# Attention and a gated MLP on one core: the weight guard on DVE, small work between DVE and GpSimd, and a new written-out order

## The chip, the cores and the metric

One Trainium2 chip, one of its cores. The metric is the device time of one execution in microseconds (us), the median of several runs. Engines are named as in the profile: PE (TensorE, matmuls; PEld its weight loads), DVE (VectorE), ACT (ScalarE), POOL (GpSimd), SP (SyncE, which issues nearly all DMAs).

## The reference

Inputs are q, k, v of shape (8, 12, 448, 64) and the weights of a gated MLP. Per batch and head:

```
q_n = q / sqrt(mean(q*q) + 1e-6) * g_q         (k likewise)
s = q_n @ k_n.T / 8;  p = exp(s - max(s));  p = p / (sum(p) + 1e-9);  a = p @ v
```

The 12 heads of a batch are laid side by side as x (448, 768). Then, per batch:

```
h = gelu_tanh(x @ w_in)                        w_in (768, 1024);  u, v = halves of h
v_n = (v - mean) / sqrt(var + 1e-6) * g_ln
out = x + (u * (w_sg @ v_n + b_sg)) @ w_out    w_sg (448, 448), w_out (512, 768)
```

The weights `w_in` and `w_out` arrive as pairs of 32-bit words, the two halves of a 64-bit float, and are decoded to fp32 on the chip.

## The kernel before

**Stages.** The kernel walks over 48 pairs of heads (`pv`, index `i`) in 24 units of four heads (index `u`). For a unit, `norms` squares q and k on ScalarE and sums them on DVE; `split` scales them on GpSimd (for unit 0 on DVE) and splits each into a high and a low fp16 half (`hl`), and two DMA transposes write them as `qt`. `scores` then makes seven score tiles for the unit, 168 in all: matmuls into a PSUM tile `s` (two buffers), the negative maximum `nm` on DVE, two exponentials on ScalarE with their sums, a fp16 high half on ScalarE (`ahl`), the low half on DVE (`ahl`, which frees the PSUM tile), and a DMA transpose into `at`. `recips` (L446) turns the sums of a pair into reciprocals: an addition of 1e-9 on DVE (`rx`, L453), the reciprocal on DVE (`ry`), and two fp16 halves on GpSimd (`rh`, `rl`). `pv` lets PE spread these over a row (`row`), multiplies attention and values, scales by the row and splits the result into fp16 halves `x`.

**Weights.** `weights` (L281) loads `w_in` in 12 pieces of 128x512 and `w_out` in 8 of 128x384. Each goes through `decode` (L259): on DVE a shift of the high word (L263) and two instructions that bring in sign and low word; on ScalarE the square of the high word read as fp32; on GpSimd a comparison of this square with a least value and a multiplication of the decoded value by the result, the guard (L267, L268). Then `w_in` is squared on ScalarE for a common scale, scaled, copied to fp16 on GpSimd, and the fp16 low part is taken on DVE (L297).

**MLP.** After each sixth pair, `moe` (for the last batch `tail`) runs the two products with `w_in`, the two gelu clusters, `layernorm` (L543), the product with `w_sg`, the gating and the product with `w_out`. `layernorm` takes the statistics on DVE and finds 1/sqrt(var + 1e-6) on DVE with a guess by integer arithmetic (2 instructions) and `newton` (7), for four columns at once.

**The order.** No engine chooses its order while running. Every operation is recorded as one entry of a plan (matmuls that belong together as one), and `Plan.emit` issues the entries in the sequence that the packed string `ORDER` gives; it was searched beforehand. Each engine, and SP's DMA queue, then works through its own instructions strictly in that order.

Of the kernel before, what the change touches and what calls it, by code (L numbers as in the profile page):

```python
# [22 lines left out]
LEAST_SQ = (1.125 * 2.0 ** -15) ** 2  # L23
# [18 lines left out]
    "44sv#i{-cJqB(la0x2|cUgl6Kp!{Ntf5o|nd(OvXHbk@MwZk^-0$+rgq~cJgI{Ey1d;QntUzWsXq|R-%d+O(ZHDK!(rKW-4RG3kfwWQ(tyCYLiZQ"
    "-gq!ubzZ^wNF2JSdZ&aoaQ@)haN@QtFs`SM}Xr^vxE=s?%Pu)!U}?wl6KM!qP1w!n4HTTcvR+7UOOKZXJ{2*i^FVW?n$4?n%1^D~^82jZK}hn*xy"
    "``@Y!GJu;NduP$A`djQW)G`!*_>>BmYld%m2BU&|qC&u2^=Z0{GC1><`VHz>)?_WMQ=Iia7hbIgi&HkMin(aR_QxyUX;aQZboe4KE&ae5<N5gVLV"
    "&i{Uw=<sKxvAHt&CK9TmbPn`q#g14xcKicJr=+J7U;6nv|*$%Kg8$s$S=0uQAK_qIj_*k<7IO69|9LsBs~*@c!%cVq4|TquHRoByx`+2J2L{d@67"
    "bAikS8B=~Jdz2TLoj9rXE=-+#Dlk8`MA-0i#&ocy5UO5?ios<|G?sq0F|t5$DRIs7L$#1xqkIsM<e&fhCobqIiujtnZ$Z+A{OI`E~PCWl_}=;+eI"
    "fe}mB1;wd8_47R&CemdA3r}U*>m%<zirwoJqRy+HoVO|cxNn4ZU*f9mzZ-^+ylv75V{B4JUbpJk|5nD=W&Wv_{Sv=VnpBeb%~j!#4ONM;qsq%w^!"
    "V*VW%ugb4QpbuLN3l3`!6Y$x-fr0b&IQGMZ2Ya(wKxfF70WrqB~g&s?(*t<3T8}i7c#Biy}+&@Lw&{-Ilg3$KJOP6XHZx1xzQwQgCe9G4Sb+OQaL"
    "4G_PpOE(@c5cY80P9niKy7qAr=rbVN2Zfdg%Gz@KeqkCwz<6|jIDAQ$25rz7!b{pI8HwP8z*n&ZVra%A#*&H^IEueL5%oXrRQ|ZAEyBeR+7@sh-V"
    "9?bdd4RFZw;+7{j~zppD>2#O#_4H~#K9J(%W+aBEk<_P86Q@>Z{Nv3_`IOSzC+-G3q%%x>;Suc%m1FbWTnAheAn_J%l|aTNjMVg(9{pqPfu~JyLc"  # L50
    "j{w?&;ZU<ZA$q4we&w>khEUjf?b#n}xnT>f)B*>ZHrj^jm9X`V|zll6=`%d#u<q6f$LF;8@hKNo_YJbACoxgzDO0_%oI<|!YT<@wt0!hivW@X{8`"
# [835 lines left out]
```

## Time and profile before

| | us |
|---|---|
| median of 3 runs (lowest to highest) | 948.27 (947.92 to 949.22) |
| the profiled execution | 948.41 |
| its span, first to last instruction | 946.6 |
| outside the span | 1.81 |

The mean granted TensorE clock was 0.949 of full speed over the span. "Busy" counts an engine's instructions alone, not its waits; an idle time is put down to the releaser that came last. The helper that records the operations stands at one line, L122, which is why nearly every row has that line: instructions are told apart by their tiles.

### The profile page before, as it was taken

The page shows a single profiled execution, that of the slowest core. Times are in us where ns is not written, and L with a number is a line of the kernel's source. Part 1 is how long each engine was busy: PE and PEld are TensorE (multiplying, and loading weights), DVE is VectorE, ACT ScalarE, POOL GpSimd, SP SyncE. Part 2 cuts the span into 40 slices and gives each one's busy share as a digit, 9 for nine tenths or more (in the row PEclk, how much of TensorE's full clock was granted, in tenths as well). Part 3 has the DMA queues.
Part 4 walks back from the last instruction along what each step waited for, and adds up shares of the span by engine and source line. Part 5 has one row for each costly group of instructions (what it writes and reads, how often), then busy time and mean ns, then how long its engine had stood idle before and what let it go on. Part 6 is the DMA issues. An engine that isn't in the chain of part 4 may idle for free.

```text
span 946.6 us, 16618 instructions
## 1 busy us (share of the span) xinstructions
PE 771.6 (82%) x5908; PEld 422.9 (45%) x5908; DVE 677.1 (72%) x1046; ACT 664.4 (70%) x1374; POOL 566.8 (60%) x669
## 2 busy tenths in 40 slices
PE   0124565797998888999898889989897999999997
PEld 0002231343454335644473347534563466444757
DVE  4988988868777786748967768559867776765052
ACT  3468866877778779767887589667877787884231
POOL 5997989885946587453865576714955762104100
PEclk9999777897899998999999899989999999999999
DMA  8966799986899889987889479959897698752102
GB/s 219 243 153 137 161 229 216 197 171 131 167 207 221 165 168 189 194 192 147 192 174 211 108 164 216 219 97 196 179 208 166 119 202 185 158 114 44 50 1 68
DMA packets 448003, 155.69 MB, mean 164 GB/s; under 512 B 404336, under 2 KB 441776, under 8 KB 447920
## 3 DMA queue, kind: packets, MB, share of 16 engines
q1 hardware_dynamic: 447344, 154.18, 76.8%
q8 instruction: 46, 0.75, 0.3%
q10 hardware_dynamic: 576, 0.46, 0.2%
q14 instruction: 37, 0.30, 0.1%
HBM read 43.57 MB, written 11.01 MB: 58 GB/s over the span
## 4 chain that ended last, share of the span: by engine, by line
PE 31%; DVE 20%; ACT 16%; POOL 12%; DMA 9%; issue 8%; SPq 4%; POOLq 0%; ACTq 0%; DVEq 0%
PE pv L122 6%; ACT s L122 5%; DVE ahl L122 4%; DVE nm L122 4%; PE s L122 4%; SPq L122 4%; DMA qt<-hl 3%; ACT ahl L122 3%; POOL qk L122 2%; POOL hl L122 2%; PE acc L122 2%; DVE vl L122 2%; ACT sqk L122 2%; DMA at<-ahl 2%; DMA qk<-in_q_dram 2%
## 5 line engine op out<-in xcount | busy, mean ns | idle before, releaser
L122 ACT ACTIVATE s<-s,nm 128x448 f32<-128x448 f32 x336 | 203.8, 607 | 73.2 <-DVE nm L122 68.5
L122 DVE TENSOR_TENSOR ahl<-s,ahl 128x896 f16<-128x896 f32 x168 | 181.9, 1085 | 69.3 <-ACT ahl L122 68.3
L122 DVE TENSOR_REDUCE nm<-s 128x2 f32<-128x896 f32 x168 | 180.9, 1085 | 41.2 <-PE s L122 40.1
L122 PE MATMUL s<-qt 64*128 64x448 f16 (+1 forms) x1152 | 134.7, 378 | 69.4 <-DVE ahl L122 58.2
L122 ACT ACTIVATE ahl<-s 128x896 f16<-128x896 f32 x168 | 153.4, 917 | 2.4
L122 PE MATMUL pv<-at,vh 128*64 128x448 f16 (+1 forms) x672 | 128.9, 382 | 18.3 <-DMA at<-ahl 7.2
L122 PEld LDWEIGHTS <-vh 128*64 128x64 f16 (+2 forms) x928 | 67.1, 110 | 113.1 <-issue 66.7
L122 PEld LDWEIGHTS <-x 128*128 128x128 f16 (+1 forms) x1056 | 74.6, 103 | 78.8 <-issue 28.8
L122 PEld LDWEIGHTS <-qt 64*128 64x128 f16 (+1 forms) x1152 | 43.1, 100 | 139.2 <-issue 95.3
L122 POOL CAST vh<-vr 128x512 f16<-128x512 f32 x48 | 30.6, 640 | 96.9 <-PE pv L122 88.6
L122 POOL TENSOR_TENSOR hl<-qk,hl 128x896 f16<-128x896 f32 x46 | 87.2, 1900 | 1.1
L122 PEld LDWEIGHTS <-wi 128*128 128x128 f16 x576 | 54.8, 99 | 61.4 <-issue 15.8
L122 POOL TENSOR_TENSOR qk<-qk,ny 128x896 f32<-128x896 f32 x46 | 78.3, 1716 | 1.6
L122 PE MATMUL pv<-at,vl 128*64 128x448 f16 (+1 forms) x336 | 74.4, 380 | 0.0
L122 POOL TENSOR_TENSOR qk<-qk,gg 128x896 f32<-128x896 f32 x23 | 49.2, 2139 | 33.3 <-ACT sqk L122 33.1
L122 DVE TENSOR_REDUCE ss<-sqk 128x14 f32<-128x896 f32 x48 | 51.8, 1079 | 21.4 <-ACT sqk L122 21.1
L122 POOL TENSOR_TENSOR gt<-gt,u 128x448 f32<-128x448 f32 x30 | 33.9, 1147 | 54.6 <-DVE gt L122 51.0
L122 ACT ACTIVATION_READ_ACCUMULATOR s<-s,nm 128x1 f32 x336 | 66.4, 198 | 0.0
L122 ACT ACTIVATE sqk<-qk 128x896 f32<-128x896 f32 x48 | 45.5, 949 | 29.7 <-DMA qk<-in_k_dram 9.0
L122 POOL CAST rh<-ry 128x8 f16<-128x8 f32 x48 | 10.5, 220 | 82.7 <-DVE ry L122 47.3
L122 POOL CAST hl<-qk 128x896 f16<-128x896 f32 x48 | 46.3, 971 | 22.1 <-DMA qt<-hl 20.3
L122 POOL TENSOR_TENSOR vl<-vr,vh 128x512 f16<-128x512 f32 x48 | 56.9, 1185 | 2.2
(834 smaller groups left out, 1747.1 us busy)
## 6 DMA issues: line engine op xcount, KB each, us to landing
out_dram<-ot SPq DMA_DIRECT2D x56, 192.0 KB, 3.0
wo_h<-in_moe_w_in_dram SPq DMA_DIRECT2D x12, 512.0 KB, 6.5
vr<-in_v_dram SPq DMA_DIRECT2D x32, 192.0 KB, 3.4
qk<-in_q_dram SPq DMA_DIRECT2D x47, 128.0 KB, 3.0
qk<-in_k_dram SPq DMA_DIRECT2D x47, 128.0 KB, 2.9
vr<-in_v_dram SPq DMA_DIRECT2D x32, 144.0 KB, 3.4
qk<-in_q_dram SPq DMA_DIRECT2D x47, 96.0 KB, 2.8
qk<-in_k_dram SPq DMA_DIRECT2D x47, 96.0 KB, 2.7
```

Of the source, the lines that this page charges most:

```text
L122: return lambda *args, **kw: self.plan.add(lambda: f(*args, **kw))
```

## The change

- `decode`: ScalarE writes the absolute value of the high word (as fp32) to the destination; a new DVE instruction takes the maximum of it and a least value; the shift then reads this result in place. The two GpSimd instructions and the square are gone.
- `w_in`'s fp16 low parts are taken on GpSimd instead of DVE (6 instructions of 128x1024).
- The addition of 1e-9 to the sums is on GpSimd instead of DVE (48 of 128x8).
- `layernorm`, except in the last batch: ScalarE's logarithm and exponential, then one step of four DVE instructions, in place of the guess and `newton`.
- `ORDER` is another sequence, for 3977 entries where there were 4018.

```diff
-LEAST_SQ = (1.125 * 2.0 ** -15) ** 2
+LEAST = 1.125 * 2.0 ** -15
 ORDER = (
...
-    def decode(dst, raw, tmp):
+    def decode(dst, raw):
         hi, lo = raw[:, :, 1], raw[:, :, 0]
-        di = dst.bitcast(I32)
-        V.tensor_scalar(out=di, in0=hi, scalar1=3, scalar2=0x3FFFFFF8, op0=ALU.logical_shift_left, op1=ALU.bitwise_and)
+        di, x = dst.bitcast(I32), raw.bitcast(F32)[:, :, 1]
+        A.activation(out=dst, in_=x, func=AF.Abs)
+        V.tensor_scalar(out=dst, in0=dst, scalar1=LEAST, scalar2=None, op0=ALU.max)
+        V.tensor_scalar(out=di, in0=di, scalar1=3, scalar2=0x3FFFFFF8, op0=ALU.logical_shift_left, op1=ALU.bitwise_and)
         V.scalar_tensor_tensor(out=di, in0=hi, scalar=-0x40000000, in1=di, op0=ALU.bitwise_and, op1=ALU.bitwise_or)
         V.scalar_tensor_tensor(out=di, in0=lo, scalar=29, in1=di, op0=ALU.logical_shift_right, op1=ALU.bitwise_or)
-        A.activation(out=tmp, in_=raw.bitcast(F32)[:, :, 1], func=AF.Square)
-        G.tensor_scalar(out=tmp, in0=tmp, scalar1=LEAST_SQ, scalar2=None, op0=ALU.is_ge)
-        G.tensor_tensor(out=dst, in0=dst, in1=tmp, op=ALU.mult)
...
-            V.tensor_tensor(out=wi[:, t, 1], in0=tmp, in1=wi[:, t, 0], op=ALU.subtract)
+            G.tensor_tensor(out=wi[:, t, 1], in0=tmp, in1=wi[:, t, 0], op=ALU.subtract)
...
-        V.tensor_scalar(out=x, in0=sums, scalar1=1e-9, scalar2=None, op0=ALU.add)
+        G.tensor_scalar(out=x, in0=sums, scalar1=1e-9, scalar2=None, op0=ALU.add)
...
-        rsqrt_guess(y, si, x)
-        newton(y, x, tt)
+        if not last:
+            A.activation(out=tt, in_=x, func=AF.Ln)
+            A.activation(out=y, in_=tt, func=AF.Exp, scale=-0.5)
+            V.tensor_tensor(out=tt, in0=x, in1=y, op=ALU.mult)
+            V.tensor_tensor(out=tt, in0=tt, in1=y, op=ALU.mult)
+            V.tensor_scalar(out=tt, in0=tt, scalar1=-0.5, scalar2=1.5, op0=ALU.mult, op1=ALU.add)
+            V.tensor_tensor(out=y, in0=tt, in1=y, op=ALU.mult)
+        else:
+            rsqrt_guess(y, sml.tile([P, CK], I32, name="li", bufs=2), x)
+            newton(y, x, tt)
```

Unpacked, the two orders put these recorded instructions ahead of some landmarks on the engine named (in brackets: how many of them belong to the decoding of the weights or its splits):

| landmark | before | after |
|---|---|---|
| GpSimd, last low half of q and k of the second unit | 64 (29) | 19 (0) |
| GpSimd, last low half of q and k of the third unit | 88 | 52 |
| DVE, first maximum `nm` | 55 (33) | 39 (24) |
| DVE, low half of the 7th score tile | 116 (44) | 95 (52) |
| DVE, low half of the 14th score tile | 144 (52) | 151 (57) |
| DVE, low half of the 21st score tile | 179 (60) | 179 (68) |
| DVE, low half of the 28th score tile | 229 (66) | 230 (80) |
| PE, score tiles ahead of the first product of the first MLP | 10 | 12 |
| PE, score tiles ahead of the first output product of the first MLP | 38 | 39 |

The number of DMA issues on SP's queue is the same, 571 recorded.

## Rows read from the trace of the kernel before

**Rows 1.** The page's first part, of the whole span: engine, busy us (share of the span), instructions.

```profile
PE 771.6 (82%) x5908; PEld 422.9 (45%) x5908; DVE 677.1 (72%) x1046; ACT 664.4 (70%) x1374; POOL 566.8 (60%) x669
```

**Rows 2.** Busy time by stretch: from and to in us from the span's start, its length, then for PE, PE's weight loads, DVE, ACT (ScalarE) and POOL (GpSimd) the busy us (instructions), the granted TensorE clock, the share of the DMA engines, GB/s.

```profile
0.00:250.00 250.00, 129.58 (x903) 57.21 (x905) 203.42 (x288) 170.14 (x356) 205.19 (x218) 0.87 0.87 185
250.00:850.00 600.00, 553.25 (x4407) 306.21 (x4405) 438.98 (x673) 464.69 (x966) 345.48 (x432) 0.97 0.83 175
850.00:947.00 97.00, 88.81 (x604) 59.44 (x600) 34.68 (x85) 29.61 (x55) 16.13 (x20) 0.99 0.19 45
```

**Rows 3.** What PE waited for from 0 to 250 us, the two longest that are used: engine, tile, the releaser, us in total, times, the longest.

```profile
PE s L122 <- DVE ahl L122: 42.4, 18, 10.5
PE s L122 <- DMA qt<-hl: 10.8, 1, 10.8
```

**Rows 4.** The same from 250 to 850 us.

```profile
PE s L122 <- DVE ahl L122: 15.7, 17, 3.4
PE row L122 <- POOL rh L122: 6.9, 4, 3.7
PE sw__1368 L122 <- DVE mv L122: 3.4, 1, 3.4
```

**Rows 5.** What DVE waited for from 0 to 250 us, the two longest.

```profile
DVE ss L122 <- ACT sqk L122: 13.2, 6, 5.0
DVE ahl L122 <- ACT ahl L122: 8.2, 11, 1.5
```

**Rows 6.** ScalarE's squares of the decoded halves of `w_in`, from the groups of instructions by shape: line, engine, operation, out<-in, shapes, count | busy us, mean ns | idle us before them and its releasers.

```profile
L122 ACT ACTIVATE wo_l<-wi 128x512 f32<-128x512 f32 x12 | 7.6, 630 | 21.2 <-POOL wi L122 21.2
```

**Rows 7.** Three pieces of the chain that ended last, between 60 and 100 us: start us, us, what.

```profile
65.08 1.50 POOL wo_l L122
78.92 1.84 POOL hl L122
80.79 5.34 DMA qt<-hl
```

**Rows 8.** DVE's and ScalarE's work on the maxima `nm` by stretch; DVE's count in brackets is the number of score tiles: length, DVE busy (count), ACT busy (count), clock, DMA share, GB/s.

```profile
0.00:250.00 250.00, 40.62 (x38) 53.72 (x151) 0.87 0.87 185
250.00:850.00 600.00, 139.24 (x129) 184.35 (x515) 0.97 0.83 175
```

**Rows 9.** GpSimd's groups of instructions by shape, those of the guard first; columns as in the group of ScalarE's squares.

```profile
L122 POOL TENSOR_SCALAR wo_l<-wo_l 128x512 f32<-128x512 f32 x12 | 18.5, 1538 | 10.9 <-DVE wi L122 9.9 <-ACT wo_l L122 0.2
L122 POOL TENSOR_TENSOR wi<-wi,wo_l 128x512 f32<-128x512 f32 x12 | 17.8, 1483 | 1.9 <-DVE wi L122 0.8 <-DVE nt L122 0.6
L122 POOL TENSOR_SCALAR sqo<-sqo 128x384 f32<-128x384 f32 x8 | 10.2, 1275 | 5.9 <-ACT sqo L122 5.4
L122 POOL TENSOR_TENSOR wr<-wr,sqo 128x384 f32<-128x384 f32 x8 | 8.0, 1002 | 4.0 <-DVE wr L122 3.8
L122 POOL TENSOR_TENSOR vl<-vr,vh 128x512 f16<-128x512 f32 x48 | 56.9, 1185 | 2.2
L122 POOL TENSOR_SCALAR nx<-ss 128x28 f32<-128x28 f32 x23 | 5.6, 242 | 5.3 <-DVE ss L122 3.6
```

**Rows 10.** DVE's groups by shape: the decode's shift (TENSOR_SCALAR) for both weights, the low parts of `w_in`, the addition of 1e-9.

```profile
L122 DVE TENSOR_SCALAR wi<-wo_h 128x512 int32<-128x512 int32 x12 | 7.3, 612 | 5.8 <-DMA wo_h<-in_moe_w_in_dram 5.8
L122 DVE TENSOR_SCALAR wr<-rawo 128x384 int32<-128x384 int32 x8 | 8.5, 1067 | 2.5 <-POOL bb L122 2.0 <-POOL wo_l L122 0.4 <-DMA rawo<-in_moe_w_out_dram 0.2
L122 DVE TENSOR_TENSOR wi<-wo_l,wi 128x1024 f16<-128x1024 f32 x6 | 7.9, 1326 | 0.0
L122 DVE TENSOR_SCALAR rx<-sums 128x8 f32<-128x8 f32 x48 | 23.0, 480 | 12.2 <-ACT s L122 12.0
```

**Rows 11.** Two lines of the answers on the tiles `wr` and `rx`: count, then shortest/median/longest in ns, first and last start in us, forms.

```profile
L122 DVE TENSOR_SCALAR wr<-rawo x8: 356/948/2219, 48.4 to 170.9; 128x384 int32<-128x384 int32 x8
L122 DVE TENSOR_SCALAR rx<-sums x48: 158/172/2858, 75.1 to 853.5; 128x8 f32<-128x8 f32 x48
```

**Rows 12.** Small instructions of the layernorm root on DVE, and the logarithm of the norms on ScalarE, from the groups by shape.

```profile
L122 DVE TENSOR_TENSOR lt<-lt,ly 128x4 f32<-128x4 f32 x16 | 4.0, 250 | 0.3
L122 DVE SCALAR_TENSOR_TENSOR ly<-lt,ly 128x4 f32<-128x4 f32 x16 | 2.6, 160 | 0.4
L122 ACT ACTIVATE nt<-nx 128x28 f32<-128x28 f32 x24 | 5.3, 221 | 9.1 <-POOL nx L122 8.9
```

**Rows 13.** Who waited for the reciprocals' two fp16 halves, whole span: PE's weight loads and PE.

```profile
PEld L122 <- POOL rh L122: 14.4, 9, 4.1
PEld L122 <- POOL rl L122: 8.3, 20, 1.9
PE row L122 <- POOL rh L122: 9.7, 7, 3.7
```

More of the change, by code (lines that the diff above doesn't have):

```diff
@@ L42 @@
[L42 to L51, printed above, removed]
@@ L97 @@
[L97 to L100 removed]
+    "c-m!G2V7Lw(!b}HU3wMiAfN~cxF86k2(}m%5i6S5dt%gRjCpy<_nBvsm(Lh`ml#W8F9^10iw!}ME+8OXK&97ZcW-;A+$Hb*KDKc8+&Ob*{xkERxh"
@@ new lines @@
+    "Cp~*J$<av7k$37I&I4*NRI{m`o`cdiR5rgkd?1e-UHRv;3G}xfoC;K8;ChlxIC|k>@)d`TcjsbH@x1)%IDJ!NT7GIQx<9p#{RZGat_vW+W~fd;i1"
+    "KPxj5^2h^AfbCPGkSHFV^YJ+cg3z)Vj?IZw8CMANo=fUMM_GjX|(%;!FocD9ax#_8AFOR%oz93<Lx*_G#+tew~bctOLA}=m_C|}t9ELOi(IBfUF^"
+    "h;oBiY)h9O;w#(e}2-R^qA!%ovy6VrVRC}4(P2;Tcy|4r_E<8(iT^FmwVPmd#Fwh9Bz^1xAz~D?zudkR9?qAue_EkaCMiz(D+Z-x8PZg_Qj!fY!L"
+    "feyZdxzh+k#mCMF^3tH4$3fM&q!1(~M~fV5HI>mli*3jG%Sk$6!knOg08%6dxVYoCkh)`R7c0^is3q_YdkP7Tq}FF1MLX_*E-Ro)@oS-^T$Qa+VF"
+    "Lz8Ll`PS-Oso=-RZOxRd+WKqd|0P+>`Cqr%q4Sa!9B=#Em!<<&d^>=y5`X&2v&v@c*IuQADm@#4!M#OveHqx;33UD(O&3}B=uHMOg@fO@9T{QoUe"
@@ new lines @@
+    "T}G-tg5i&@@<*W`3ucamw1ZwQ7jjySfn)JMwTqW0h5-V`pUaFQ0ASyg#G>d~!H6*Uay^cI<<wyr}z5-Wi*A#5^9wNhTc=pA?4jl$KR<_hLDaHPoc"
+    "N?ERFW;%ieZ9!8palmu*>*1|_L>P%CHIot_%JCmqyv$oVWrYEwOX4`b1|IngRb8vJp=&}-7Ak07C%-JMfXsvXzu+7?@BvpjXW{#%J?zps2bupnd="
+    "&F!%Y2WGv3CT&z<2qL?KF8;lcFaA$LVdu#6<8!*p0ywrxYgSYD!FQL=v?}~tD2VTt0%9`yy6CS&35O6dR<CP<j-I6yW+Vi%Nkt4rl5P@4Xn5y`?q"
+    "&XVttdweL282ZTp`StWP{O=?c_)J(f&Qf3)@M@e{tR8}$9%ypWQ{@3)*<Fgi^;v3&J+(YMV{EFV#zJ+$eY6*9APlYNBu0as0mjg3ZPQtU^ky0x2b"
+    "{^`iZ^<TQL-@AT`)_pzr-pY4!S&EL1$P3kr=0JR|9+ErjW)LrM>by{yc9sX3+{+HTIA{EI&w+nVPO*IP^^Md?PbT;G-8J0t`V`0Pg7Bcmffco5pB"
@@ new lines @@
+    "g;gc)Yo^kUzJf-Ed}Zw;dC;a<0>!MS^6w0_HFPFnSi8PV8_v7w1;P0`m@z1%T74fK9j7^PR0p&4q<BcYL9Bk9{M@v*w)?XC>&ZnjAa4n?=E-Gd#n"
+    "-Q{AtL?Pb&kvo1qa9?+<A{mVN?@{5m`Xo`M3QR2@QJQx?umkFAD_U^_!m4A^q+z@i+&Nxw%v#jXH%_UdAP7cWfv-!e`Qok8LZPmXrMDRa;anmEzB"
+    "rD|y!;jwrA#a4kjwSX@8LtB(q~}rKN&F3YRQgETs-q~#>b7N2c-Eu1^bjCCjrA|d4z|8&)f#)quV3fnZT@odO1bmqN0vK2<4tvquEUmW*uARJyDE"
+    "8x^E;2-GwqW;J+vllX~MLn3HGgYTuww96Y$yLTL~`7kyn}NJ%zj02UK_eYuNOBZB+ZKpeu{+S&1Wae%>GqGtKE8b!K|LYS=Sj|M_fM4l1(kU@bh0"
+    "e_d$T&Iw1?fbbl(fBwLiBU9sgYPJ5aLvz2mP*dsjcBb&aIY{W5yQ6IEoO?0sJt1}M^m`_`q2|1txvXI5^EPjx&V{$Gv@`8`8EMwh#8|f8pCt7=Gh"
@@ new lines @@
+    "cNaEImFj?7V6o*Q0Kb-A;Vauhos}Y4uQ70Jk1<V33+!c)?QF<jPB8yL(-5eJe;=z_vN-+lI92fr{_6R`Kk6|Mq$l-maOGV(e1wqKn@jU28A_k*WQ"
+    "}c1OLvNt0DTCZqLi7Ki76Q1E=$`Qoh?iUJ;tQ>CcK?Fr$c?iX(qc884LIc(&;k^z>nY*zTKyuaTn2%RWrF5PPxF{Els*o0d%GKSuF&}59t4ZS;A$"
+    "O`98Z!Z4z1J9P^cs7|~C$g#2gqt9qk*qz6>7araW3<c#_c85<HeQ@@**!{aNY7ZGbNu8Z;cf8FrTzVnd;I>T)W#-ROs`$?m=%9pRr=`5_S(5iqy3"
+    "Y>Dz5b2ug{K+4nD9}CzUMDI=Z4HBe6QLObj?OdMIBS!~-*4C=4o=!)zO0j=wv!0Kh+yrCqGJLNQn@jcs;ltsd5tmkXAKzq%jJ%Gr@(_@d8;zIr?&"
+    "BxcW+e`+Ikscxt286WgK>YCTayHy}%rQ3<%E-TNy2^T(pn|CN_)!{sg34-t{m=#lJ*#0(S+c(dbZJDpFD45-Q!@Vx3&@J-vP)}A>GO%Lt=d;v$zl"
@@ new lines @@
+    "xF}g4wCb4MPn%!*Yt2_q+_%R)h+@<sX;i`k3l~C2g+tz7X>`JZqR+Y8Wg_Hf;p|E*bn<)G@{&njKhrEULcJt4;u`?o`oh4+`{%hPZ>&^30d64eoU"
+    "#{Exde$n^00R$##&_Uc!k{jns~f`98$?%oRQTg}w%wtB&~k!E?DPS&i;o~LxCobci8iZyx7z`toJ$W|L}`L{Ru4dibIc;?v*zCKaK-=4~(OteVld"
+    "S|8z@uKMs9XnB-JoAPqdp3-JB*aOE`|P}XA#~38?qs(A_%<$ND?K3>fQZa@&b6M<npOXp(^jO(A9DZBUY)6Cw8f0G6C8$C`fQwB{(8~SFJkK>Ge?"
+    "Sbf3EEbQt?+GZQOMzz46Yv!%<v(Sr?~cPaMn@>J5o6xTBMLRc_3$pNN{maxj1uS<ze{AQsjH4q!m)5QElSH06Q5a$Hky#n>kA)M=G|;8HxeI=y^Q"
+    "xxHP5Ofy#gZSOk|ooH<B^m@&CE&Csz>Vs>5CZG37i_eOBpBCTf_+;#uy=9~3J-l@AtnHNF9fc3iJ~7wMgxqO!%}3MpWb_j_IZSWLOymtx-iUJ_N#"
@@ new lines @@
+    "{Ky0*m#H-oE)<or6Us^EmOnEctY{Ik8&vM<WewZf`u_0N`EaYT(|w)xR1GbXGO4vH<`y0kArj6W(~!70zB6K9zyG3bl=cO^zgZRIz@&^&YQ%E1g?"
+    "poiE^fqHhh*h2DsJ98lan{nGi<H_u$W>d~T2$az!kHStcZ=hXan70Vu##QGib@qD<>aCGgpiFe}j?tYu8k^c2fF|WzZi%1?c_%_$;rQu)I3SJs@_"
+    "YHRHE&UAcO5C++oB&@A&CjMbgN(X4s?)1m!~Z_x!pFju@4j`3X3wzw&BydyoSxRAcQvbdyY7)$Z@ybU5dCyQk#~*|VR|fmLPE9>Su^0%#D*xZhvy"
+    "c$W<2^rp8RI1#cb=IsKPuS*>?M)*!!oW(+1SQe3*ZFM0Vu-6O3m}an9qUN33lZuem1r3e^u|e1)0^D_}z_9#S}XP^n2#ph03(e7P7@7%ZC@Y_+*V"
+    "PA#%|9QMNp5ier4uP_6EH&|@>V7Q^+_78Tc)9OwA=zFdj9sMq(@OAeGuKD&y);8O?<>f5<ZL-iD_<N|+tx~@br+>{oACfn5(n;S3ZQ}rBwp;T$wB"
@@ new lines @@
+    "|Q8u30Ygw}%B6j%hv@D7^yR&fNiKp-*f5df7@JmA2LgFpf25Ows7pu3A5?aENG<KdRfi$^Wg(i(GHl9T6Z{>(pYFo3Y3wpYiQcm4)Vd$#(5_xgK>"
+    "I&?D(Bdg|l>wE_o#Q?1(Ry*vNjSuXK^=lrhA%0+tbRATE~6yQ*1aPC(osB~)I=5`&ewrPx0kGN(Pdu&jK=;v%`ZL_n_aIkX}xW`c(^MK=e$D|3->"
+    "@$7rgXoOW%tJQniHEmjaVOfW_sQt=XiyULXH<C*Us@kyp(_RNoZoo(mw-`icj%|zKALr&k1KSwZ1mvmy7N}1!|31q`ot*iA<*1%2|cptx1>Cg&3R"
+    "wBp*Jt;(yc=|Ry$YO=CiIxHVrxBX?ytN20n4gB*slJIk5V@>jAK_=jfV)Nw0RTKB8L4fkSH~O{ymyyedwf_EHFZW$IN@<<IZl@G`(u)(2h)3Ml6T"
+    "xQl@~^Dj*U$unA71~ZM|R=9(Ib92*Z_}Tt<VcUsvA!#RgEpUUr{N**IK3JaCO+#!_XBCyix4-`O4%hTJW)648;nLxA_I%fi>Gf{ChLXrS`-_VhS("
@@ new lines @@
+    "~@4STYPN=`uA~R66!(-MDIr>DTI^Z?rqTgslgzH4YYXy<?M$;py1A>+${AM`d8DbJF6IYYr|{@!VS%wQSo+Ili&9egE6U0YbgkzNxMaz{{%P*jj_"
+    "5iN2vRF;f>)_td*vZ&%M-+c(&7^*%cn^cTbOI;~56>ixI=p{mai=KW#SW#v^kv#bilf!i^U#*|f0HIxN~rH?!wET_&f+z{p%O8iTMFZ&L@?o%6gy"
+    "EjgCO^8#e&a-TS;rdkd*_ptU7n40l3gB|0O~?6}CKlHl*qLc@-2vYTiKrsSWNO#$fA7@j*ytFYS^fRr=F__CZ=!VS5#<5=&hh$C)6-rNs}HJ94&u"
+    "lCrg9ngLlhfx-Kwk6(XwJtsM!+}!zk@#KSSBz+IcTPp)ahY`~ZVRPFzj#Kns@^gP}Bxe;Jq;@oYqP&?_-0Z+K34R;cyv<+Q*=6!~XoeJVY4)JD9>"
+    "pw?!aZ2m5Sc@Cb^pC_Iv4zBF6NJ(&Ks|Sh&p}%a{xfuv1V%D<Deu2kq26E*-g*{=GIyg=i2T57+)h~x<hxHauZV`KnBQl3^FT%1l9Anvy#`w&UX8"
@@ L101 @@
+    "1IUL`*iwL{yPVJ&>^CzDC52NkQQ@gTsoXmH7yd$jUGx(n>!>=u<=u>2{briEi9M$pzKN62^W>NPv($<_Hu(3<r>9V-YJZ5T>Dw^Sw+MObHN4U_gq"
+    "D%nC$OCOk+{#xYNMx>3e0NqO!g&qy*LWUJHzAR{K#M{`)X?+KA2RR*NKCrDD(q)32lJVquhM0x(i6Bh}pGSDf_QaOZDEKtHo8An6%A3q%tAO4yR|"
+    "DrOb?NfcI{@2HtKL0UX8vo?J9rAxE_)Fh^|C9gUKl$H%80GW"
 )
@@ L288, in weights @@
             dst = wi_f[:, j // 2, (j % 2) * WC:(j % 2 + 1) * WC]
-            decode(dst, raw.rearrange("p (a b) -> p a b", b=2), work[:, 2 * DF + j % 2 * WC:2 * DF + (j % 2 + 1) * WC])
+            decode(dst, raw.rearrange("p (a b) -> p a b", b=2))
             A.activation(out=work[:, j % 2 * WC:(j % 2 + 1) * WC], in_=dst, func=AF.Square, accum_out=part[:, j:j + 1])
@@ L328, in weights @@
             wr = mlp.tile([P, EH], F32, name="wr", tag="gt", bufs=NOT)
-            sq = mlp.tile([P, EH], F32, name="sqo", tag="ug", bufs=5)
-            decode(wr, raw, sq)
+            decode(wr, raw)
             A.activation(out=wo_h[:, t, es], in_=wr, func=AF.Copy)
@@ L378, in norms @@
             skv = sk[:, 0:SSW * D].rearrange("p (c d) -> p c d", d=D)
-            A.activation(out=skv, in_=U[u]["qk"][:, x].rearrange("p h c d -> p (h c) d"), func=AF.Square)
+            z = U[u]["qk"][:, x].rearrange("p h c d -> p (h c) d")
+            A.activation(out=skv, in_=z, func=AF.Square)
             V.tensor_reduce(out=ss[:, x], in_=skv, axis=AX.X, op=ALU.add)
@@ L527, in pv @@
         xh, xl = (x_all[:, i % NX, n] for n in range(2))
-        V.tensor_tensor(out=ps, in0=ps, in1=row, op=ALU.mult)
-        A.activation(out=xh, in_=ps, func=AF.Copy)
-        V.tensor_tensor(out=xl, in0=ps, in1=xh, op=ALU.subtract)
+        x = ps
+        V.tensor_tensor(out=x, in0=ps, in1=row, op=ALU.mult)
+        A.activation(out=xh, in_=x, func=AF.Copy)
+        V.tensor_tensor(out=xl, in0=x, in1=xh, op=ALU.subtract)
         XT[i] = (xh, xl)
@@ L559, in layernorm @@
         x = sml.tile([P, CK], F32, name="lx", bufs=2)
-        si = sml.tile([P, CK], I32, name="li", bufs=2)
         y = sml.tile([P, CK], F32, name="ly", bufs=2)
```

74 lines of the change are left out of this document (20 added, 54 removed).

## The prediction, made before the change was run

> **What bounds the kernel now.** I read the busy shares first. DVE is busy 677.1 us of the 946.6 us span and GpSimd 566.8 us, PE 771.6 us [rows 1]; no engine fills the span, so the average says little and I cut the span into stages. In the first 250 us PE is busy for only 129.6 us, while DVE (203.4) and GpSimd (205.2) are both full to about 82%; from 250 to 850 us PE works 553.25 of 600 us and DVE 439; in the last 97 us PE works 88.8 and DVE 34.7 [rows 2]. So two limits follow one another: a first stage in which DVE and GpSimd decode the weights and feed the first score tiles, and a long stage that PE nearly fills. A saving on DVE or GpSimd is worth something in the first, little in the second, nothing in the last.
>
> Next, what PE waits for. Up to 250 us it is above all the second half of a score tile (DVE's subtraction `ahl` frees the two PSUM buffers) and one wait of 10.8 us for the first transposed q and k [rows 3]. From 250 to 850 us the same wait on `ahl` is only 15.7 us, the row of reciprocals 6.9 us, the layernorm's statistics 3.4 us [rows 4]: PE is idle for 600 − 553.25 = 46.75 us there, and these three are 26.0 of it.
>
> What feeds the first stage? DVE is idle for 250 − 203.4 = 46.6 us of it, 13.2 us of this waiting for ScalarE's squares of q and k and 8.2 us for ScalarE's fp16 halves [rows 5]. ScalarE itself waited 21.2 us for GpSimd's guarded weights before it could square them [rows 6], and q and k are squared in the same queue. And the chain that ended last runs through GpSimd: at 65 us a guard comparison, at 79 us the split of q for the second unit of four heads, then its transpose, which lands at 86 us, with k's still to come [rows 7]. By 250 us 38 of the 168 score tiles have passed, against 129 in the next 600 us [rows 8]: 6.6 us a tile against 4.65.
>
> **The change, part by part.**
>
> *The guard.* GpSimd loses all four groups: 18.5 + 17.8 + 10.2 + 8.0 = 54.5 us [rows 9]. ScalarE's 20 squares become 20 absolute values of the same shapes; I take their price as equal. DVE gains 20 `max` instructions, and its shift now reads the tile just written instead of the strided high words. No row shows this `max`. The nearest is the shift itself, also one input, same tile: 612 ns for 512 elements and 1067 ns for 384 [rows 10], so at the upper end 12 × 0.612 + 8 × 1.067 = 15.9 us. At the lower end stands the fastest shift, 356 ns for 384 [rows 11]: 8 × 0.356 + 12 × 0.356 × 512/384 = 8.5 us. I take 12, the middle. Why is the mean of that row three times its fastest? Fastest 356, median 948, slowest 2219 ns, with the same work each time: it stands waiting for something. The sums' addition has the same face: 158, 172, 2858 ns [rows 11].
>
> The Trainium skill has a rule for it (SBUF — State Buffer, "Who interferes with whom"): a DVE `tensor_scalar` in its two-port mode and any GpSimd instruction exclude each other for a whole instruction, whichever started first. The spread of these rows agrees with it. The rule speaks against this part: it puts 20 more such instructions into a stage in which GpSimd is busy; I make it a rival below. By the Trainium skill (ScalarE: Activation LUTs, "Table sets") the absolute value is in every table set, so it asks for no table load; no run here shows this yet.
>
> *w_in's low parts.* DVE loses 7.9 us [rows 10]. GpSimd has no such row of 1024 elements; its subtraction of 512 takes 1185 ns [rows 9], so 6 × 2 × 1.185 = 14.2 us.
>
> *The sums.* DVE loses 48 × 480 ns = 23.0 us [rows 10], of which 48 × 172 ns = 8.3 is work and 14.7 waiting [rows 11]. GpSimd gains 48 instructions at the price of a small one, 242 ns [rows 9]: 11.6 us. What is queued behind: on GpSimd the addition now waits for the last exponential of a pair of heads, and the splits of q, k and v stand behind it; then `rh` waits, as now, for DVE's reciprocal.
>
> *The layernorm root.* Seven times nine small DVE instructions become four, and two go to ScalarE. Five fewer at 160 to 250 ns [rows 12] are 0.8 to 1.25 us each time, 5.6 to 8.8 in all; I take 7. ScalarE gains 14 × 221 ns = 3.1 us [rows 12]. One hop to ScalarE and back is added, hidden behind score work unless the two stand late in its queue.
>
> So DVE goes down by 23.0 + 7.9 + 7 − 12 = 25.9 us, GpSimd by 54.5 − 14.2 − 11.6 = 28.7 us. In the first stage alone (all the weights, about 11 of the 48 additions, one layernorm): DVE −7.9 − 5.3 − 1 + 12 = −2.2 us, with bounds −5.7 (8.5 for the guard) and +1.7 (15.9); GpSimd −54.5 + 14.2 + 2.7 = −37.6 of 205.2 us.
>
> *The order.* Unpacked, it moves about half of the instructions, by few places each. Its first stage differs in kind. The last split of the second unit stood 65th on GpSimd behind 29 weight instructions, and stands 20th behind none; the first score tile's maximum was 56th on DVE, and is 40th. But by the 21st tile both programs have put 179 DVE instructions ahead, and by the 28th 229 and 230: what is won by starting early is paid on DVE, where all decoding is still ahead of the 28th tile. All loads and transposes go through SP's queue in the same number, 571. The first PE work of the first MLP stands two score tiles later (behind the 12th instead of the 10th), its output products one tile later.
>
> **The sum.** First stage: DVE's own work −2, and of its 46.6 us of idle time I take away 10. The reason: ScalarE no longer waits for a GpSimd guard, and the GpSimd chain to the second unit is shorter by 29 instructions; but the wait for the first data stays. Together −12; bounds +2 (idle stays, dear guard) and −27 (the 21.4 us of both waits gone and 5.7 of work). From 250 to 850 us: DVE is relieved by some 24 of 439 us and three waits of PE hang on it, 26.0 us; I take 4, bounds 0 and 26. Last stage: 0, its layernorm keeps the old root. The new order beyond this: 0, since no row prices it; as an estimate up to 9 us either way, a fifth of PE's 46.75 us idle. The profiled execution took 948.41 us, the median of the three runs is 948.27, so nothing need be shifted: 948.4 − 12 − 4 = **932 us**.
>
> **The rivals.**
>
> *The additions stall in GpSimd's queue* (slower). Each row of reciprocals gets one more GpSimd instruction, and GpSimd works in order: a split in front costs up to 1.84 us [rows 7], on average half, plus 0.24, so 1.16 us. PE already stands at these rows now: 7 waits of `row` for `rh`, 9 and 20 of the weight loads for `rh` and `rl` [rows 13], so 16 to 36 of the delays could reach it. 14 of them eat up the 16 us won; with 26 it is 26 × 1.16 − 16 = +14, 962 us; with all 36, 974. Against it: GpSimd has 254.5 us free from 250 to 850, and `rl` waits of PE's loader are short.
>
> *The port.* If each of the 40 tensor_scalars (`max` and shift) waits as the 384 wide one does, 1.067 − 0.356 = 0.71 us, DVE gets 28 us of waits where the 20 shifts now have about 8 × 0.71 + 12 × 0.14 = 7 (0.14 is 0.612 less the fastest shift scaled to 512 elements, 0.356 × 512/384). The first stage then has −14.2 for what leaves DVE (7.9 + 5.3 + 1), 8.5 for `max` at its fastest and 28 − 7 = 21 of waits, +15 us on its bound, its idle time stays, and with −4 later it is 959 us. This is the rule named above. Against it: GpSimd is the emptier by 37.6 us in that stage, and the waits shrink with it.
>
> *DVE was the bound of the first stage all along*, and the same amount of work by the 28th tile means the same time: with nothing from the middle, 948 ± 2. For it speaks the equal count; against it the 46.6 us idle.
>
> *More*: both early waits gone (−27) and half of the middle's 26.0 (−13): 908 us.
>
> **How the numbers follow.** The forecast of 932 (its own range 920 to 944) gets 0.52, the larger gain 0.10, no effect 0.12, the stalled additions 0.18, the port 0.08. Faster by over 0.2% (1.9 us, about what a measurement tells from no change) is 0.52 + 0.10 = 0.62, within it 0.12, slower 0.18 + 0.08 = 0.26. The range goes down to 912, which leaves out most of the larger gain, and up to 960, which leaves out the upper half of the two slower cases.
>
> **What would show it.** Right: the second unit's q transposed by about 60 us instead of 86, over 40 tiles by 250 us, GpSimd near 538 us and DVE near 651 us busy, table loads still 30. Wrong: `rx` on GpSimd long after the last exponential and PE's waits for `rh` above 30 us (the first rival); `max` and shift of `wi` and `wr` at 1 us or more on average (the second); the same 38 tiles at 250 us with DVE over 90% busy there (the third).

## The result, and the profile after

The changed kernel takes 919.07 us (median of 4 runs, 917.42 to 920.54); the ratio to the kernel before, measured beside it, is 0.9708 (95% interval 0.9675 to 0.9742). That is 29 us less against a forecast of 16 less: the direction and the range of 912 to 960 hold, the size was nearly twice as large, and the forecast's own range, 920 to 944, was missed by a microsecond. The profiled execution took 917.42 us, its span 915.6.

The stages first, in the columns of [rows 2]:

```profile
0.00:250.00 250.00, 148.95 (x1035) 69.89 (x1036) 210.75 (x297) 182.05 (x381) 180.45 (x211) 0.85 0.91 199
250.00:850.00 600.00, 560.52 (x4470) 309.80 (x4469) 433.14 (x631) 466.07 (x979) 359.09 (x470) 0.99 0.82 172
850.00:916.00 66.00, 59.41 (x408) 43.74 (x406) 19.71 (x49) 14.52 (x29) 2.89 (x2) 0.98 0.17 43
```

The third stretch ends with the program. In the first 250 us PE was busy for 19.4 us more than in [rows 2] (1035 instructions against 903), with GpSimd 24.7 us emptier and DVE 7.3 us fuller; in the next 600 us PE was busy for another 7.3 us more. The score tiles, in the columns of [rows 8]:

```profile
0.00:250.00 250.00, 44.19 (x41) 58.88 (x164) 0.85 0.91 199
```

41 against 38. What moved in the first stage is seen in three places. First, PE's first score matmuls wait in both kernels for the transposed q and k of the first unit, and these come 16 us sooner (the kernel before, then the changed one):

```profile
50.79 2.42 PE L122 MATMUL s<-qt 64*128 64x448 f16 x12 [10.83 <-DMA qt<-hl]
```

```profile
34.56 2.42 PE L122 MATMUL s<-qt 64*128 64x448 f16 x12 [11.65 <-DMA qt<-hl]
```

Ahead of them PE waits for loads of v, which is PE's second longest wait of the first 250 us before; [rows 3] doesn't show it. It is 12 us shorter now (again the kernel before, then the changed one):

```profile
PE psv L122 <- DMA vr<-in_v_dram: 33.3, 3, 16.2
```

```profile
PE psv L122 <- DMA vr<-in_v_dram: 21.3, 2, 20.4
```

Second, GpSimd's low halves of q and k (start, us, engine, line, operation) come at 43 to 47 us for the second unit, where [rows 7] had the first of them at 79:

```profile
42.96 4.17 POOL L122 TENSOR_TENSOR hl<-qk,hl 128x896 f16<-128x896 f32 x2
```

Third, ScalarE, which waited 21.2 us for GpSimd's guard before it could square [rows 6], no longer waits for it at all (the same group after):

```profile
L122 ACT ACTIVATE wo_l<-wi 128x512 f32<-128x512 f32 x12 | 7.5, 622 | 3.6 <-DVE wi L122 3.6
```

The prices that [rows 9, 10, 12] bounded, as measured: the maximum of `w_in` and of `w_out`, the two shifts behind them, then on GpSimd the low parts and the addition, then one small DVE instruction of the new root:

```profile
L122 DVE TENSOR_SCALAR wi<-wi 128x512 f32<-128x512 f32 x12 | 5.9, 495 | 6.5 <-ACT wi L122 6.4
L122 DVE TENSOR_SCALAR wr<-wr 128x384 f32<-128x384 f32 x8 | 6.9, 865 | 0.5 <-ACT ny L122 0.4
L122 DVE TENSOR_SCALAR wi<-wi 128x512 int32<-128x512 int32 x12 | 7.0, 593 | 0.2
L122 DVE TENSOR_SCALAR wr<-wr 128x384 int32<-128x384 int32 x8 | 4.4, 555 | 0.1
L122 POOL TENSOR_TENSOR wi<-wo_l,wi 128x1024 f16<-128x1024 f32 x6 | 12.7, 2127 | 0.2
L122 POOL TENSOR_SCALAR rx<-sums 128x8 f32<-128x8 f32 x48 | 13.0, 271 | 70.6 <-ACT s L122 60.5 <-ACT ly L122 8.0
L122 DVE TENSOR_TENSOR ly<-lt,ly 128x4 f32<-128x4 f32 x7 | 2.8, 404 | 0.2
```

GpSimd stands 60.5 us waiting for the last exponential ahead of `rx`, as foreseen; the question is who waits for GpSimd then. PE and its loader, in the columns of [rows 13]:

```profile
PEld L122 <- POOL rh L122: 19.9, 10, 5.2
PEld L122 <- POOL rl L122: 4.5, 13, 1.2
PE row L122 <- POOL rh L122: 11.9, 7, 4.4
```

Together 36.3 us against 32.4; the waits for `rh` alone went from 24.1 to 31.8 us, while those for `rl` became shorter.

### The profile page after: what moved, and what is told of

It is laid out like the page before. It is cut to its first block, busy times and chain, and to the rows that moved or that the text cites. A ratio compares the mean times of both kernels' runs of the same rounds, so it can differ in the third digit from the quotient of the medians.

```text
span 915.6 us, 16548 instructions
## 1 busy us (share of the span) xinstructions
PE 768.9 (84%) x5908; PEld 423.4 (46%) x5908; DVE 663.6 (72%) x977; ACT 662.6 (72%) x1388; POOL 542.4 (59%) x683
## 4 chain that ended last, share of the span: by engine, by line
PE 38%; ACT 15%; DVE 13%; POOL 6%; issue 6%; DMA 3%; SPq 1%; ACTq 0%; DVEq 0%; POOLq 0%
PE pv L122 7%; ACT s L122 5%; PE s L122 5%; DVE nm L122 4%; DVE ahl L122 3%; ACT ahl L122 3%; PE acc L122 3%; PE row L122 2%; POOL hl L122 1%; ACT L122 1%; SPq L122 1%; ACT sqk L122 1%; DVE vl L122 1%; ACT vg L122 1%; DMA at<-ahl 1%
## 5 line engine op out<-in xcount | busy, mean ns | idle before, releaser
L122 PE MATMUL s<-qt 64*128 64x448 f16 (+1 forms) x1152 | 132.0, 373 | 50.5 <-DVE ahl L122 37.9
L122 PE MATMUL pv<-at,vh 128*64 128x448 f16 (+1 forms) x672 | 131.6, 390 | 16.4 <-DMA at<-ahl 6.4
L122 POOL TENSOR_TENSOR qk<-qk,gg 128x896 f32<-128x896 f32 x23 | 48.4, 2103 | 24.1 <-ACT sqk L122 23.3
L122 POOL TENSOR_SCALAR rx<-sums 128x8 f32<-128x8 f32 x48 | 13.0, 271 | 70.6 <-ACT s L122 60.5
```

The source lines that it names most:

```text
L122: return lambda *args, **kw: self.plan.add(lambda: f(*args, **kw))
```

## The experiments

All are given with the ratio to the kernel before, which ran beside each on the same chip; differences between kernels of different groups are read from these ratios as well (0.01 is 9.5 us). The changed kernel's ratio is 0.9708 (0.9675 to 0.9742).

| kernel | what differs from the changed kernel | median us | ratio (95% interval) |
|---|---|---|---|
| o_before | old order, all four edits | 944.82 | 0.9987 (0.9957 to 1.0018) |
| u_all | new order, no edit | 953.84 | 1.0075 (1.0041 to 1.011) |
| u_guard | guard back on GpSimd | 950.3 | 1.0052 (1.0027 to 1.0076) |
| u_guard_wi | the same for `w_in` alone | 935.72 | 0.9865 (0.9829 to 0.9901) |
| u_rx | addition back on DVE | 921.36 | 0.9751 (0.9693 to 0.981) |
| u_wlow | low parts back on DVE | 921.62 | 0.9741 (0.9697 to 0.9785) |
| u_ln | old layernorm root | 926.84 | 0.9779 (0.9749 to 0.981) |
| u_three | the last three together | 931.03 | 0.9833 (0.9779 to 0.9888) |
| h_early | new order to tile 41, then old | 934.38 | 0.9879 (0.9833 to 0.9924) |
| h_late | old order to tile 41, then new | 934.49 | 0.9888 (0.9839 to 0.9936) |
| h_late_three | h_late without the three edits | 943.94 | 0.9946 (0.9922 to 0.9971) |
| h_100 | new order to tile 100, then old | 922.48 | 0.9732 (0.9687 to 0.9777) |

**Edits or order?** `o_before` sorts the changed kernel's operations by their places in the old order; `u_all` keeps the new order and undoes the four edits.

```diff
 # o_before
-ORDER = (new)
+ORDER = (old; new instructions at the place of those they replace)
```

> All four edits of the changed kernel, but issued in the order of the kernel before (each new instruction at the place of the one it replaces; the maximum right ahead of the shift). Theory A (the edits carry the gain, above all the guard's leaving GpSimd in the first 250 us): most of the 29 us stays, 922 to 932 us. Theory B (the new order carries it): 938 to 948 us. Under A the second unit's splits on GpSimd finish well ahead of the 86 us of before although the order is the old one; GpSimd is then idle or waiting at 40 to 80 us.

```diff
 # u_all: decode
-        A.activation(out=dst, in_=x, func=AF.Abs)
-        V.tensor_scalar(out=dst, in0=dst, scalar1=LEAST, scalar2=None, op0=ALU.max)
-        V.tensor_scalar(out=di, in0=di, scalar1=3, ...)
+        A.activation(out=tmp, in_=x, func=AF.Square)
+        V.tensor_scalar(out=di, in0=hi, scalar1=3, ...)
...
+        with plan.group():
+            G.tensor_scalar(out=tmp, in0=tmp, scalar1=LEAST_SQ, scalar2=None, op0=ALU.is_ge)
+            G.tensor_tensor(out=dst, in0=dst, in1=tmp, op=ALU.mult)
 # and rx, w_in's low parts and the root as before
```

> The new order with all four edits undone: guard on GpSimd, low parts of w_in and the addition of 1e-9 on DVE, layernorm root by guess and Newton steps. (The entries of the order keep their number: operations that have no entry of their own stand together with a neighbour; the square for w_out is written over the raw high words.) Theory A: 940 to 950 us, the gain is gone. Theory B: 920 to 930 us, most of it stays.

Neither theory holds for both runs: `o_before` lies where theory B put it, `u_all` a little above where theory A put it. The edits in the old order give nothing that can be told from no change, and the new order without the edits is 0.75% slower than the kernel before. Why the old order can't use the edits shows in `o_before` on GpSimd: its queue is empty of guards, yet the second unit's low halves still come at 74 and 79 us,

```profile
74.03 1.88 POOL L119 TENSOR_TENSOR hl<-qk,hl 128x896 f16<-128x896 f32 x1
79.11 1.88 POOL L119 TENSOR_TENSOR hl<-qk,hl 128x896 f16<-128x896 f32 x1
```

against 43 us in the changed kernel. (My placement has a part in it: there DVE waits 18.6 us for ScalarE's absolute values, 6.4 us in the changed kernel.)

**The guard.** `u_guard` undoes the guard alone, as in the diff above; `u_guard_wi` does so for `w_in` only.

> The changed kernel with the guard alone put back to GpSimd (comparison and multiplication there, behind the last instruction of each decoding; the square for w_out is written over the raw high words), new order. GpSimd gets 54 us back, DVE loses 24 us. Theory A: +10 to +18 us over the changed kernel, that is 929 to 937, as GpSimd's splits of q and k stand behind guards again. Theory B: +0 to +5, 919 to 924.

> The changed kernel with the guard of w_in alone put back to GpSimd (24 instructions, 36 us); w_out keeps the new guard. If what counts is GpSimd's queue ahead of the second unit's splits and ahead of the first MLP: +15 to +28 us, 934 to 947, most of the 31 us of both guards, and the first product of u moves from 176 us to 190 or later. If all guards count alike by their time (36 of 54 us): +18 to +22; if w_out's guards, which stand later, matter more: +5 to +12.

The guard alone takes back the whole gain in the new order, 0.034 of the time, about twice what I expected even under theory A; `w_in`'s guard takes 0.016 of it, just under half, where I expected most. `w_out`'s share, the rest, is less sure: in `u_guard` its square stands two DVE instructions later. Both guards also stand where I put them, behind each decoding, in an order that was made without them; a better place in the same order was not tried. Where the loss goes: ScalarE waits for GpSimd again, before the squares of `w_in` and before the copies of `w_out` (ScalarE's groups in `u_guard`; the second shows 2.6 us of idle time in the changed kernel).

```profile
L122 ACT ACTIVATE wo_l<-wi 128x512 f32<-128x512 f32 x12 | 7.5, 624 | 19.6 <-POOL wi L122 19.6
L122 ACT ACTIVATE wo_h<-wr 128x384 fp32r<-128x384 f32 x8 | 4.2, 520 | 13.8 <-POOL wr L122 13.8
```

ScalarE's queue holds the exponentials and the squares of q and k as well, so all of them stand behind these waits. GpSimd's own queue is longer too: the second unit's low halves still come early in `u_guard` (47 us), the third's at 96 us, where the changed kernel has 78; and DVE's reciprocals wait for the addition of 1e-9, which now stands behind guards in GpSimd's queue (first 250 us of `u_guard`; 3.4 us in the changed kernel; 7.3 us of the wait for `wi` stand before other work than the squares):

```profile
DVE ry L122 <- POOL rx L122: 18.9, 5, 5.2
ACT wo_l L122 <- POOL wi L122: 27.4, 10, 7.3
ACT wo_h L122 <- POOL wr L122: 13.8, 6, 4.0
```

In `u_all` the addition is on DVE, so that the first of these waits can't arise. ScalarE's waits are the same there,

```profile
ACT wo_l L122 <- POOL wi L122: 26.3, 9, 7.3
ACT wo_h L122 <- POOL wr L122: 14.9, 6, 4.0
```

and the product looked at next starts at the same time, so the loss doesn't hang on the addition. What ScalarE's waits and the later splits cost one by one, these runs don't part. The loss is complete by the first MLP. Its first product with u's half of `w_in` starts at (the kernel before, the changed one, `u_guard`, `u_guard_wi`, `o_before`, `u_all`):

```profile
197.75 2.43 PE L122 MATMUL mu__335<-x,wi 128*128 128x448 f16 x12
```

```profile
176.50 2.22 PE L122 MATMUL mu__326<-x,wi 128*128 128x448 f16 x6 [1.70 <-ACT vg L122]
```

```profile
204.67 2.40 PE L122 MATMUL mu__326<-x,wi 128*128 128x448 f16 x6 [1.02 <-ACT vg L122]
```

```profile
193.66 2.40 PE L123 MATMUL mu__326<-x,wi 128*128 128x448 f16 x6 [2.26 <-ACT vg L123]
```

```profile
193.94 2.43 PE L119 MATMUL mu__326<-x,wi 128*128 128x448 f16 x12
```

```profile
204.07 2.40 PE L122 MATMUL mu__327<-x,wi 128*128 128x448 f16 x6 [1.48 <-ACT vg L122]
```

The same instruction, 28.2 and 17.2 us late in the two kernels with an old guard alone: about what they lose at the end (0.034 and 0.016 of 948 us are 32.6 and 14.9). It is waiting, not slower matmuls. Up to this product, in the columns of [rows 2] (the kernel before, the changed one, `u_guard`),

```profile
0.00:197.75 197.75, 86.34 (x604) 37.85 (x604) 161.76 (x221) 130.88 (x276) 166.56 (x170) 0.88 0.88 189
```

```profile
0.00:176.50 176.50, 84.73 (x577) 36.80 (x577) 153.59 (x220) 127.16 (x268) 122.09 (x140) 0.85 0.96 212
```

```profile
0.00:204.67 204.67, 86.43 (x577) 37.76 (x577) 152.29 (x201) 127.14 (x268) 171.32 (x178) 0.82 0.81 184
```

PE was busy only 1.7 us longer in `u_guard` than in the changed kernel, for the same 577 instructions.

How guard and order need each other shows in the score tiles passed (DVE's counts on `nm`, added up) and in the start of the first `nm`:

```
score tiles by      50   100   150   200   250 us    first nm
kernel before        0     8    18    29    38           52.8 us
changed kernel       3    12    23    31    41           35.9
u_guard              3     9    18    28    36           36.1
o_before             0    10    18    30    40           52.8
```

The new order brings the early start, whichever guard it has. With the old guard the lead is gone by 150 us; with the new one it is kept. In the old order there is no early start to keep.

**First stage or whole run?**

```diff
 # h_early / h_late / h_100
-ORDER = (new)
+ORDER = (new up to the low half of score tile 41, then old)   # h_early
+ORDER = (old up to the low half of score tile 41, then new)   # h_late
+ORDER = (new up to the low half of score tile 100, then old)  # h_100
```

> The changed kernel's operations, in the new order up to the low half of the 41st score tile (about 250 us), from there in the order of the kernel before. Both orders have done the same operations by that tile but for 14. Theory A2 (the gain of edits and order together is made in the first 250 us): 919 to 928 us. Theory C (it is made along the whole run, by the order of the middle too): 930 to 937 us.

> The other half: the order of the kernel before up to the low half of the 41st score tile, from there the new order. Theory A2: 936 to 946 us, little better than the edits in the old order (944.8). Theory C: 928 to 935 us.

> The changed kernel's operations, in the new order up to the low half of the 100th score tile (about 520 us) and from there in the order of the kernel before. In h_early (old order from the 41st tile on, 934.4 us) the fourth MLP starts its statistics 12.6 us later than in the changed kernel. If this is time lost and the middle's gain is made between the 41st and 100th tile: 919 to 925 us. If it is only another place of the same work and the gain is spread over the middle: 926 to 931 us.

My second theory, that all of it is made in the first 250 us, fell as well: each half of the new order alone gives about 0.010 over the old one, both together 0.028. `h_100` says where the middle's share is made: with the new order up to tile 100 all but 0.0024 is there (its interval overlaps the changed kernel's). In `h_early` the statistics of the fourth MLP start 12.6 us late (505.5 us against 492.9). From 250 us up to them, in the columns of [rows 2], `h_early` and the changed kernel:

```profile
250.00:505.50 255.50, 230.43 (x1828) 126.93 (x1827) 178.29 (x259) 198.43 (x413) 157.52 (x207) 0.97 0.87 182
```

```profile
250.00:492.90 242.90, 225.48 (x1827) 125.17 (x1826) 179.73 (x255) 194.71 (x411) 161.16 (x206) 0.99 0.90 190
```

PE ran as many instructions but for one. Of the 12.6 us, 7.6 are idle time of PE (25.1 against 17.4 us), and 5.0 are longer busy time, with a mean granted clock of 0.97 against 0.99; whether the idle time brings the lower clock the runs don't show. The largest of the waits, in the same two stretches:

```profile
PE s L118 <- DVE ahl L118: 11.7, 8, 2.1
```

```profile
PE s L122 <- DVE ahl L122: 7.3, 9, 2.4
```

That is 4.4 us of the 7.6; the rest is spread over several releasers. No single wait was removed by the order.

**The three smaller edits.**

```diff
 # u_rx
-        G.tensor_scalar(out=x, in0=sums, scalar1=1e-9, scalar2=None, op0=ALU.add)
+        V.tensor_scalar(out=x, in0=sums, scalar1=1e-9, scalar2=None, op0=ALU.add)
 # u_wlow
-            G.tensor_tensor(out=wi[:, t, 1], in0=tmp, in1=wi[:, t, 0], op=ALU.subtract)
+            V.tensor_tensor(out=wi[:, t, 1], in0=tmp, in1=wi[:, t, 0], op=ALU.subtract)
 # u_ln: the six entries of the new root hold the nine old instructions
-            A.activation(out=tt, in_=x, func=AF.Ln)
-            A.activation(out=y, in_=tt, func=AF.Exp, scale=-0.5)
...
+            V.tensor_scalar(out=si, in0=x.bitcast(I32), scalar1=1, ...)
+            V.tensor_scalar(out=y.bitcast(I32), in0=si, scalar1=-1, scalar2=MAGIC, ...)
...
```

> The changed kernel with the addition of 1e-9 put back to DVE, new order. Theory A: DVE gets up to 48 x 0.48 = 23 us back, of which some 15 are waits, mostly in the middle stage where PE hides them: +2 to +6 us, 921 to 925. Rival (the hop over GpSimd costs more than it saves, since GpSimd stands waiting for the last exponential for 60 us in all): 0 to -5 us, 914 to 919.

> The changed kernel with the low parts of w_in alone put back to DVE, new order: GpSimd loses 12.7 us between the 12th and 21st tile, DVE gets about 8. If GpSimd is what holds up the first stage there: -2 to -6 us, 913 to 917. If DVE is: +3 to +8 us, 922 to 927.

> The changed kernel with the layernorm root alone put back to guess and Newton steps on DVE, new order. The three edits cost 12 us together when undone, the additions 2.3 and the low parts 2.6 of them. If the three simply add up: +5 to +9 us, 924 to 928. If it is DVE's total load that counts and not the part: +1 to +4, 920 to 923, and the three are worth more together than singly.

> New order and new guard; the other three edits undone (low parts of w_in and the addition of 1e-9 on DVE, layernorm root by guess and Newton steps). Theory A2 (guard and order make the gain between them): 919 to 927 us. Rival (the three moves off DVE, 38 us of its work, carry a third or more of the gain): 930 us or more.

> The order of the kernel before up to the 41st score tile and the new order from there (as h_late, 934.5 us), with the three smaller edits undone. If the middle's 10 us come from the order alone: 934 to 940. If the order pays there only with the work taken off DVE: 942 to 950.

Singly the additions and the low parts are not told from nothing (their intervals overlap the changed kernel's, though both medians are 2.3 and 2.6 us above); the root is worth 0.0071, 6.7 us; all three 0.0125, 11.9 us, about as much as the three medians' differences add up to (2.3 + 2.6 + 7.8 = 12.7), and over a third of the gain, as the rival to theory A2 had it. In `u_ln` the time on DVE from the start of the root's first instruction (`lx`) to the end of its last (`ly`), read off the timeline, is 47.0 us over the seven MLPs, and 39.2 in the changed kernel, whose order is the same: 7.8 us shorter. The start of the layernorm's statistics falls behind, but not evenly:

```
MLP                 1      2      3      4      5      6      7      8
changed kernel  176.5  292.9  409.8  492.9  600.8  693.0  805.8  870.9 us
u_ln            177.8  297.6  414.3  497.5  605.6  699.6  813.4  878.8
u_guard         204.7  323.3  439.4  522.5  631.9  723.1  836.5  901.5
```

`u_guard`'s lag is there from the first MLP, 28 us, and stays near 30; the root's grows from 1.3, which is there before any root has run, to 7.9. It grows by 3.4 behind the first MLP, 1.8 behind the fifth and 1.0 behind the sixth, whose roots are 2.1, 1.8 and 2.0 us longer in `u_ln`; behind the other four, whose roots are 0.4 to 0.6 us longer, by 0.3 at most. So the longer chain reaches PE in three of the seven MLPs. Not all of the 7.9 us is waiting for it, either: PE's busy time for the same 5908 instructions is 773.2 us in `u_ln` and 768.9 in the changed kernel.

`h_late_three` undoes the three edits under the new middle order: 0.9946 against 0.9888 for `h_late`, with intervals that overlap a little. What the three are worth in the old middle order was not run, so it is not shown that the order pays there only with them.

None of these versions is faster than the changed kernel.

## Why the prediction was right, and where its sizes were off

**The stages** were read rightly. The first stage's term named two causes, the end of ScalarE's wait for the guard [rows 6] and a shorter GpSimd chain to the second unit [rows 7], and the runs show that neither brings it by itself. In `o_before` ScalarE's wait is gone and the chain as late as before: 3.8 us are won by the first MLP's product. In `u_guard` the chain is early and the wait is back: 6.9 us are lost against the kernel before. With both, 21.3 us are won (197.75 to 176.50). The term was mis-sized: −12 was put there. Up to that product DVE's idle time fell by 13.1 us (36.0 to 22.9), where I took away 10, and its busy time by 8.2, where I had 2. One of its premises was wrong: "the wait for the first data stays". The first score matmuls start 16 us sooner, in `u_guard` too (34.80 us), so this is the order's doing; I had the first maximum moved from the 56th to the 40th place on DVE in front of me and gave it no price.

**DVE's own work** in the first stage was guessed well: `max` cost 5.9 + 6.9 = 12.8 us (12 taken), while the shifts fell from 15.8 to 11.4. Over the whole span DVE went from 677.1 to 663.6, not to 651: three of its four small root instructions now take about 0.4 us where [rows 12] had 0.16 to 0.25, and the root's instructions together 12.0 us where they had 14.1 (all eight MLPs), so that 2 us of busy time were saved and not 7. GpSimd is at 542.4 (538 foreseen), table loads stayed at 30.

**The middle's term** was mis-sized: −4 was put there, and 9.7 us were won behind the first MLP's product (31.0 us of span less 21.3). The root was put down as 7 us of DVE's busy time within this term; it saved 2 us of that, and undoing it costs 6.7 us of the program. A busy time saved in a stage that PE fills is worth little only where it isn't a link of the chain to the next PE work; in three of the seven MLPs this one was.

**The order** is the step that failed as such: 0, ± 9 us, "since no row prices it". The sum gives the edits 16 us and the order none; the edits without the order bring 0.9987, the order without the edits 1.0075, and both together 0.9708. It is no term of a sum, since a freed queue is worth what is put there. That the time came out in the forecast's direction is therefore in part luck: the sum credited the edits with what they bring only in an order that uses them, and this order does. The table of places said as much (the second unit's splits from the 65th to the 20th place) and I used it for the mechanism without giving it a price.

**The rivals.** The stalled additions: the sign that I had named for them, more than 30 us of waits for `rh`, was met (31.8). With the addition back on DVE, in `u_rx`, these waits are 25.1 us,

```profile
PEld L122 <- POOL rh L122: 15.5, 8, 5.1
PE row L122 <- POOL rh L122: 9.6, 5, 4.3
```

and `u_rx` is still not faster than the changed kernel. So the delay is there, some 7 us of waits of PE and its loader, and costs no more than the move saves. The port: the maximum of `w_out` still takes 865 ns on average, where the fastest of its maxima and shifts takes 335,

```profile
L122 DVE TENSOR_SCALAR wr<-wr x16: 335/360/2080, 53.6 to 182.4; 128x384 f32<-128x384 f32 x8, 128x384 int32<-128x384 int32 x8
```

but the median of these 16 is 360, where the eight shifts of before had 948 [rows 11], and GpSimd was emptier, as the argument against this rival had it. The few long ones are of the kind that the rule of the Trainium skill (SBUF — State Buffer, "Who interferes with whom") would give, an instruction held up by the whole of another. No run here parts this from other causes. These waits were no reason to leave the guard on GpSimd. That DVE bounds the first stage all along: it was busy 210.75 us there, 84%, and 41 tiles passed instead of 38, so no. *More* (908 us) lay a little closer to the result than the forecast did.

What stays open: which of the order's moves between tiles 41 and 100 shorten the waits there, and what the granted clock has to do with it; why the two halves of the order give 0.021 by themselves and 0.028 together; how much of `w_out`'s share of the guard is due to the later square in `u_guard`; and how the guard's cost divides between ScalarE's waits and GpSimd's own queue.

## What to carry to other kernels

Price a moved instruction by the queues of the engines that wait for its result, and not by its own time alone: the guard on GpSimd put waits into ScalarE's queue, which also holds the exponentials. Where the order is written out by hand or searched, edits and order are one change: neither showed a gain without the other, so an edit that "does nothing" in the old order isn't refuted. And a chain of tiny instructions ahead of each stage can be worth its length in time, even where its engine is a quarter idle: here 6.6 us came behind roots that were 7.8 us longer in all.

## What the runs showed of the hardware

A busier PE was granted less of its clock in one stretch and more in another (means over the stretch). From 50 to 100 us, in the columns of [rows 2], the changed kernel and the kernel before:

```profile
50.00:100.00 50.00, 25.62 (x167) 10.80 (x167) 48.78 (x77) 40.17 (x82) 37.40 (x40) 0.81 0.98 216
```

```profile
50.00:100.00 50.00, 16.75 (x95) 7.19 (x94) 43.50 (x65) 38.54 (x80) 43.70 (x44) 0.95 0.62 141
```

From 150 to 200 us, the same two:

```profile
150.00:200.00 50.00, 40.77 (x260) 17.61 (x259) 40.72 (x68) 39.63 (x83) 41.75 (x46) 0.90 0.91 198
```

```profile
150.00:200.00 50.00, 35.27 (x263) 15.23 (x257) 39.24 (x61) 39.48 (x83) 43.08 (x50) 0.83 0.94 186
```

PE is busy for 25.62 us at 0.81 against 16.75 at 0.95 in the first, and for 40.77 at 0.90 against 35.27 at 0.83 in the second. Over the first 250 us it is 0.85 against 0.87, and PE still ran more instructions; over the whole span it is 0.949 in both.

Busy time is not a fixed price, either. `o_before` and the changed kernel have the same instructions in two orders:

```profile
PE 768.8 (82%) x5908; PEld 422.7 (45%) x5908; DVE 636.7 (67%) x977; ACT 665.8 (71%) x1388; POOL 530.3 (56%) x683
```

```profile
PE 768.9 (84%) x5908; PEld 423.4 (46%) x5908; DVE 663.6 (72%) x977; ACT 662.6 (72%) x1388; POOL 542.4 (59%) x683
```

The same 977 DVE instructions were busy for 26.9 us longer in the order whose span is 27.7 us shorter; the root's first multiplication (`lt` from `lx` and `ly`) took 418 ns on average against 171. What holds them up was not tested.
